# An attention and token/channel mixer kernel: the first batch written out by hand on three engines

## The chip, the cores and the metric

The kernel runs on one core of a Trainium2 chip. The metric is the device time of one execution in microseconds (us). Five engines take part: PE (matrix multiplications), DVE (VectorE), ACT (ScalarE), POOL (GpSimd) and SP, which here only issues DMA transfers. Each engine works through its own list of instructions in order and waits on semaphores for the others.

## The reference

Eight batches, 576 positions, 8 heads of 64. Attention runs inside chunks of 64 positions; its result x goes through a token mixer (along positions) and a channel mixer, each with a residual.

```python
# q, k, v: float32 (8, 8, 576, 64), in chunks of 64
scores = scale * np.matmul(q_c, k_c.transpose(0, 1, 2, 4, 3))
scores = scores - np.max(scores, axis=-1, keepdims=True)
attn = np.exp(scores)
attn = attn / (np.sum(attn, axis=-1, keepdims=True) + 1e-09)
out = np.matmul(attn, v_c)                    # -> x (8, 576, 512)
# w_tok1 (576, 256), w_tok2 (256, 576), w_ch1 (512, 1536), w_ch2 (1536, 512): float64
h = np.maximum(xt @ w_tok1, 0.0) @ w_tok2     # xt: x with positions last
u = x + h.transpose(0, 2, 1)
h2 = np.maximum(u @ w_ch1, 0.0) @ w_ch2
return u + h2
```

The four weight matrices arrive as float64 and are turned into float32 on the chip.

## The kernel before

**Tiles.** Two batches share nine attention tiles of 128 rows: batch 0 has five (the fifth is half its own, half batch 1's), batch 1 four, and so on in pairs. Per tile: scores (`attn_s`, L215, 32 small matmuls), on DVE a maximum (L223) and a subtraction (L225), on ACT the exponential (L229), a transposition of the probabilities `pr` to `pt`, the values with an added column of ones (`attn_v`, L276), and on DVE the division (`zi` L284 and L285, then `x` L287). The first batch transposes on PE (`near`, L254, copied by ACT at L267); later tiles go through a block transposition on DVE (L235), a DRAM buffer (`far`) and back (`pf`, `xt`).

**Mixers.** Of batch 0 the token mixer uses plain float32: `tok1_first` (L363) sums over the five tiles, a relu gives two halves of `r`, `tok2_first` adds the residual x to the same accumulator with identity matmuls (L378), multiplies `r` by the second weight (L385) and splits the result u into a rounded part `uh` (ACT, L389) and a remainder `ul` (DVE, L390). From there on, and in all later batches, a product of two float32 values is three matmuls of high and low parts (`THREE`). The channel mixer works on two halves of 288 positions in 12 steps: `ch1` (L432, 12 matmuls), the relu split into `gh` (ACT, L439) and `gl` (DVE, L440), and `ch2` (L459, 12 matmuls) into four accumulators, which step 11 adds to u (L466) and sends out. For batch 0, `ch1` of both halves runs in the first pass, with the second half's `gh` and `gl` kept; its `ch2` steps follow in a second pass. Batch 1 begins with `tok2` (L412).

**Weights.** A plan lists 31 pieces: three of the first token weight (t1), four of the second (t2), 24 of the channel weights (c1, c2 in turn, 512 columns each). A piece is fetched as pairs of 32-bit words (`fetch`, issued by SP), and converted by `convert_words`: two ACT passes (L138 the low words, L144 the magnitude of the high words), then on DVE a clamp (L145), a shift (L148), the sign (L152) and an addition (L156). `convert_split` rounds it to a high part on ACT (L170) and subtracts it on DVE (L171); the results are `kept_c` and `kept_t`. Batch 0's token mixer reads the float32 pieces (`tops`), the channel mixer and later batches read the split ones. The t pieces' splits are called in the second pass of batch 0.

**What sets the order.** SP's order is that of the program. For the first stage PE's order is too: the table `FIRST` says for each of seven steps how many weights to fetch, how many pieces to convert, and how many warming matmuls (L101, on zeros, results unused) to run ahead of the transposition and of `tok1_first`. DVE, ACT and POOL there, and every engine but SP afterwards, are ordered by a planner from its own estimates of durations. `qk` and `v` have three buffers each, so the load of the fourth tile waits for the first's to be free.

## Time and profile before

| what | value |
|---|---|
| median of three runs | 845.03 us (844.12 to 845.63) |
| the profiled execution | 846.61 us |
| its span in the trace | 844.8 us |
| mean granted clock of PE in it | 0.982 |
| PE busy | 824.5 us, 98% of the span |
| DVE busy | 358.1 us, 42% |
| ACT busy | 233.3 us, 28% |
| POOL busy | 116.4 us, 14% |
| first score matmul | 5.89 us |
| last x of batch 0 done | 49.34 us |
| first channel matmul | 63.95 us |
| last channel weight's remainder written | 113.40 us |
| first output addition of batch 0 | 135.84 us |
| first token-mixer matmul (L412) of batch 1 | 166.23 us |

A row of the profile names the line of the kernel (L276), the engine, the operation, what it writes and reads (out<-in) and how often it occurs; busy times are in us. Idle time of an engine is put down to what came last before it went on. Busy shares are averages over the whole span, so the stages are looked at one by one. The granted clock is 1.00 at full speed.

### The profile page before, as it was taken

How to read it: one execution, taken by the hardware profiler on the slowest of the kernel's cores; microseconds unless marked ns; L12 is line 12 of the kernel's file. 1: busy time of each engine (PE TensorE's matmuls, PEld its weight loads, DVE VectorE, ACT ScalarE, POOL GpSimd, SP SyncE). 2: the span in 40 equal slices, each digit the busy share in tenths (PEclk: the TensorE clock that was granted, in tenths of full speed). 3: DMA queues.
4: the chain of work that ended last, by engine and by line, in shares of the span. 5: the costliest groups of instructions: out<-in, count | busy, mean ns of one | idle time of the engine just before them, and what ended most of it. 6: DMA issues, size and time to landing. Idle time of an engine off the chain costs nothing.

```text
span 844.8 us, 18037 instructions
## 1 busy us (share of the span) xinstructions
PE 824.5 (98%) x7632; PEld 769.5 (91%) x7632; DVE 358.1 (42%) x762; ACT 233.3 (28%) x479; POOL 116.4 (14%) x133
## 2 busy tenths in 40 slices
PE   8689999999999999999999999999999999999997
PEld 5358999899998999999998999989999899999997
DVE  5989963253335334143433433243333434223121
ACT  4667731132223222132222322122222322212110
POOL 0000002220203002030201202030120302014000
PEclk8769999999999999999999999999999999999999
DMA  7891133323433233212433234202334223200000
GB/s 282 332 383 32 64 108 111 96 74 111 133 97 110 87 108 117 63 55 88 139 129 101 75 122 136 77 29 95 107 121 139 74 90 101 91 15 15 2 29 29
DMA packets 69985, 87.97 MB, mean 104 GB/s; under 512 B 8016, under 2 KB 48208, under 8 KB 69904
## 3 DMA queue, kind: packets, MB, share of 16 engines
q1 hardware_dynamic: 69904, 86.82, 31.2%
q8 instruction: 60, 0.98, 0.5%
q14 instruction: 21, 0.17, 0.1%
HBM read 59.92 MB, written 25.95 MB: 102 GB/s over the span
## 4 chain that ended last, share of the span: by engine, by line
PE 91%; DVE 4%; DMA 2%; ACT 2%; issue 0%; SPq 0%; DVEq 0%; ACTq 0%
PE acc L459 37%; PE ps_c L432 36%; PE ps_t L354 6%; PE ps_t L412 6%; PE ps_s L215 3%; PE ps_v L276 2%; DMA raw_t<-in_w 1%; DVE wtop L152 1%; PE ps_t L378 1%; DVE kept_c L171 1%; ACT low L138 1%; DVE wtop L145 1%; DVE wtop L156 0%; DMA raw_c<-in_wc 0%; DVE wtop L148 0%
## 5 line engine op out<-in xcount | busy, mean ns | idle before, releaser
L432 PE MATMUL ps_c<-uh,kept_c 128*128 128x288 f32 x1536 | 316.9, 296 | 0.0
L459 PE MATMUL acc<-gh,kept_c 128*128 128x288 f32 x1536 | 297.1, 297 | 1.4 <-ACT gh L439 1.3
L432 PEld LDWEIGHTS ps_c<-uh,kept_c 128*128 128x128 f32 x1536 | 247.0, 188 | 2.2
L459 PEld LDWEIGHTS acc<-gh,kept_c 128*128 128x128 f32 x1536 | 237.6, 188 | 5.8 <-ACT gh L439 2.9
L432 PE MATMUL ps_c<-ul,kept_c 128*128 128x288 f32 x768 | 226.4, 297 | 0.8 <-DVE ul L390 0.8
L440 DVE SCALAR_TENSOR_TENSOR gl<-ps_c,gh 128x288 fp32r<-128x288 f32 x192 | 86.9, 453 | 306.2 <-ACT gh L439 305.8
L459 PE MATMUL acc<-gl,kept_c 128*128 128x288 f32 x768 | 201.1, 296 | 0.0
L439 ACT ACTIVATE gh<-ps_c 128x288 fp32r<-128x288 f32 x192 | 78.8, 411 | 343.7 <-PE ps_c L432 332.4
L432 PEld LDWEIGHTS ps_c<-ul,kept_c 128*128 128x128 f32 x768 | 143.7, 188 | 1.4 <-DVE ul L390 1.0
L459 PEld LDWEIGHTS acc<-gl,kept_c 128*128 128x128 f32 x768 | 136.0, 189 | 0.8
L305 POOL TENSOR_TENSOR xl<-x,xh 128x512 fp32r<-128x512 f32 x28 | 36.8, 1313 | 401.4 <-ACT xh L304 387.1
L468 POOL TENSOR_TENSOR o<-o,ul 128x288 f32<-128x288 f32 x56 | 43.4, 803 | 234.0 <-DVE o L466 233.9
L412 PE MATMUL ps_t<-kept_t,rh 128*128 128x288 f32 x224 | 46.6, 302 | 0.0
L423 ACT CAST uh<-u 128x288 fp32r<-128x288 f32 x56 | 23.9, 432 | 47.8 <-DVE u L418 47.7
L354 PE MATMUL ps_t<-xh,kept_t 128*128 128x512 f32 x112 | 36.8, 405 | 0.0
L263 ACT COPY pt<-pf 128x512 f32<-128x512 f32 x31 | 19.2, 620 | 63.2 <-DMA pf<-far 63.2
L223 DVE TENSOR_REDUCE mx<-ps_s 128x8 f32<-128x512 f32 x36 | 24.8, 688 | 27.9 <-PE ps_s L215 27.8
L412 PEld LDWEIGHTS ps_t<-kept_t,rh 128*128 128x128 f32 x224 | 35.4, 188 | 1.0
L229 ACT ACTIVATE pr<-pr 128x512 f32<-128x512 f32 x36 | 22.7, 632 | 45.4 <-DVE pr L225 45.2
L215 PEld LDWEIGHTS ps_s<-qk 64*64 64x64 f32 x1152 | 24.1, 138 | 10.7 <-issue 8.4
L276 PE MATMUL ps_v<-v,pt 64*64 64x65 f32 x1152 | 26.9, 233 | 6.6 <-ACT pt L267 6.5
L412 PE MATMUL ps_t<-kept_t,rl 128*128 128x288 f32 x112 | 33.2, 301 | 0.0
(62 smaller groups left out, 631.2 us busy)
## 6 DMA issues: line engine op xcount, KB each, us to landing
qk<-in_qk SPq DMA_DIRECT2D x36, 512.0 KB, 3.9
far<-blocks SPq DMA_DIRECT2D x63, 256.0 KB, 2.1
raw_c<-in_wc SPq DMA_DIRECT2D x24, 512.0 KB, 9.5
v<-in_v SPq DMA_DIRECT2D x36, 260.0 KB, 4.2
out<-o SPq DMA_DIRECT2D x64, 144.0 KB, 1.9
pf<-far SPq DMA_DIRECT2D x124, 64.0 KB, 2.0
xt<-far SPq DMA_DIRECT2D x112, 64.0 KB, 2.0
raw_t<-in_w SPq DMA_DIRECT2D x4, 288.0 KB, 4.8
```

What stands on the lines that cost most here:

```text
L215: nc.tensor.matmul(ps[c * CH:(c + 1) * CH, a, hp * CH:(hp + 1) * CH], lhsT=qk[a * D:(a + 1) * D, 0, hp, c * CH:(c + 1) * CH], rhs=qk[a * D ...
L223: nc.vector.tensor_reduce(out=mx, in_=sv, axis=AX.X, op=ALU.max)
L276: nc.tensor.matmul(ps[c * CH:(c + 1) * CH, a, hp * DV:(hp + 1) * DV], lhsT=t["pt"][a * CH:(a + 1) * CH, hp, c * CH:(c + 1) * CH], rhs=t["v ...
L305: nc.gpsimd.tensor_tensor(out=xl, in0=t["x"], in1=xh.bitcast(F32), op=ALU.subtract)
L354: nc.tensor.matmul(ps, lhsT=lhsT, rhs=rhs, start=(n == 0 and q == 0), stop=(n == len(mt) - 1 and q == len(terms) - 1),)
L412: nc.tensor.matmul(ps[:, :HALF], lhsT=r[k][ri][:, m * P:(m + 1) * P], rhs=weights["t2", k, n][:, wi], start=(k == 0 and q == 0), stop=(k = ...
L423: nc.scalar.copy(out=uh[:, m], in_=u)
L432: nc.tensor.matmul(ps[:, :HALF], lhsT=weights["c1", f][:, wi, k * P:(k + 1) * P], rhs=u[ui][:, k], start=(k == 0 and q == 0), stop=(k == N ...
L439: nc.scalar.activation(out=gh, in_=ps[:, :HALF], func=AF.Relu)
L440: nc.vector.scalar_tensor_tensor(out=gl, in0=ps[:, :HALF], scalar=0.0, in1=gh.bitcast(F32), op0=ALU.max, op1=ALU.subtract)
L459: nc.tensor.matmul(accs[e], lhsT=weights["c2", f][:, wi, e * P:(e + 1) * P], rhs=g[gi], start=(f == 0 and q == 0), stop=(f == NFC - 1 and ...
L468: nc.gpsimd.tensor_tensor(out=o, in0=o, in1=u[1][:, e].bitcast(F32), op=ALU.add)
```

## The change

The first batch, up to the token mixer's first half, is written out in order for PE, ACT and DVE, not for PE alone. A generator, `conversion()`, yields one DVE step of the weight conversion at a time; the steps of two to three neighbouring pieces are interleaved (clamp of piece i, sign of piece i-1, shift of i, addition of i-1, remainder of i-2). `convert(n)` places the next n of them, and tables give the number at each place: `FIRST_FILL` per tile, `END_FILL` behind the last tile, `STEP_FILL` in the channel steps. `prepare` places the two ACT passes of a piece, and each such pass fetches the piece five further on (`AHEAD`). Warming matmuls go from 68 to 20.

Batch 0's x is transposed on PE into `xt` (copied by ACT), and batch 0 uses the general `tok2`, with DVE adding `xt` to the accumulator (`u`); the identity matmuls of `tok2_first` are gone. Tiles 0 to 4 get five buffers for `qk` and `v` of their own, later ones two. Steps that belonged to batch 1's attention are placed in the channel steps of batch 0 by a table of slots (`JOBS`, two slots per step in the first pass, one in the second). The seven splits of t pieces come at slots 25 to 31 and not ahead of the last instruction of the first pass on ACT and DVE. After the part written by hand the planner orders the three engines again, with nothing ahead of its end.

```diff
-FIRST = (
-    (2, 1, 0, 12),
-    (1, 1, 10, 2),
-    (2, 1, 8, 0),
-    (2, 1, 4, 0),
-    (2, 1, 4, 0),
-    (2, 1, 4, 4),
-    (1, 1, 0, 0),
-)
+AHEAD = 5
+WARM_T = (6, 2, 0, 0, 0)
+WARM_V = (0, 0, 0, 0, 0)
+FIRST_FILL = (3, 4, 5, 5, 6)
+PREPARE = (0, 2, 2, 2, 2)
+X_BEFORE = ((), (), (0,), (1,), (2,), (3, 4))
+END_FILL = (4, 3, 1)
+STEP_FILL = (5, 5)
+STARTS = ((10, 11, 13, 14), (15, 16, 18, 19), (20, 21, 24, 25), (25, 27, 30, 31))
+JOBS = [(9, "ready")]
+JOBS += [(s, "part", j, k) for j, ss in enumerate(STARTS) for k, s in enumerate(ss)]
+JOBS += [(25 + i, "split", i) for i in range(7)]
...
+    fetched = []
     def fetch(n):
-        for i in [j for _, j in zip(range(n), fetched)]:
+        for i in range(len(fetched), min(n, len(plan))):
+            fetched.append(i)
             key, src, lo, n = plan[i]
             nc.sync.dma_start(
                 out=raws[i][1].rearrange("p n w -> p (n w)"), in_=src[:, lo:lo + n].bitcast(I32)
             )
...
+    def words_scalar(i):
+        fetch(i + AHEAD)
+        n = plan[i][3]
+        st = raws[i][1]
+        tag, bufs = (f"wt{n}", token) if i < token else ("wt", 4)
+        tops[i] = pool.tile([P, n], F32, tag=tag, name="wtop", bufs=bufs)
+        lows[i] = pool.tile([P, DM], I32, tag="low", name="low", bufs=4)[:, :n]
+        nc.scalar.activation(out=tops[i], in_=st[:, :, 1].bitcast(F32), func=AF.Abs)
+        nc.scalar.activation(out=lows[i], in_=st[:, :, 0].bitcast(U32), func=AF.Copy, scale=2.0 ** -29)
...
+    prepared = []
+    def prepare(n=1):
+        for _ in range(n):
+            if len(prepared) < len(plan):
+                words_scalar(len(prepared))
+                prepared.append(len(prepared))
+    def conversion():
+        for i in range(len(plan) + 2):
+            if i < len(plan):
+                prepare(i + 1 - len(prepared))
+                words_clamp(i)
+                yield
+            if 0 < i <= len(plan):
+                words_sign(i - 1)
+                yield
+            if i < len(plan):
+                words_shift(i)
+                yield
+            if 0 < i <= len(plan):
+                words_add(i - 1)
+                if i - 1 >= token:
+                    split_high(i - 1)
+                yield
+            if token <= i - 2:
+                split_low(i - 2)
+                yield
...
-        qk = pool.tile([P, 2, NHP, P], F32, tag="qk", name="qk", bufs=3)
+        qk = pool.tile([P, 2, NHP, P], F32, tag="qk" if i > 4 else "qk0", name="qk", bufs=2 if i > 4 else 5)
...
+    def attn_p(i, fill=0):
+        t = tiles[i]
+        sv = t["s"]
         mx = pool.tile([P, 2, NHP, 1], F32, tag="mx", name="mx")
         nc.vector.tensor_reduce(out=mx, in_=sv, axis=AX.X, op=ALU.max)
-        pr = pool.tile([P, DM], F32, tag="pr", name="pr")
+        convert(fill)
...
+    def attn_o(i, fill=(0, 0)):
+        t = tiles[i]
+        pv = t["pv"]
         zi = pool.tile([P, 2, NHP, 1], F32, tag="zi", name="zi")
         nc.vector.tensor_scalar_add(out=zi, in0=pv[:, :, :, D:], scalar1=1e-9)
+        convert(fill[0])
         nc.vector.reciprocal(out=zi, in_=zi)
...
+            dst = xt[:, 4 * j:4 * j + (rows.stop - rows.start) // BK]
+            if ps is None:
+                far_in(tiles[t]["x"], dst, rows)
+            else:
+                nc.scalar.copy(
+                    out=dst.rearrange("p i n c -> p n i c"),
+                    in_=near(tiles[t]["x"], ps).rearrange("p (n q) -> p n q", n=NDT)[:, :, rows]
+                    .rearrange("p n (i c) -> p n i c", c=BK),
+                )
...
+            terms = [(r[k], tops["t2", k, n])] if b == 0 else [
+                (r[k][ri], weights["t2", k, n][:, wi]) for wi, ri in THREE
+            ]
...
+        while ("c1", f) not in weights:
+            convert(1)
...
+    by_hand = ExitStack()
+    by_hand.enter_context(tc.manual_schedule(engines=engines))
...
+    fetch(2)
     load_v(first[1])
-    with tc.manual_schedule(engines={nc.tensor.engine}):
-        warm(20)
-        sums = [ps_sum.tile([P, 512], F32, tag="sum", name="sum") for _ in range(NT1)]
-        for step, (weights_in, finish, warm_t, warm_x) in enumerate(FIRST):
-            i, j, k = step, step - 1, step - 2
-            fetch(weights_in)
-            if i + 2 < len(first):
-                attn_load(first[i + 2])
-            warm(warm_t)
-            if 0 <= j < len(first):
-                attn_t(first[j], ps_tr.tile([P, 512], F32, tag="t", name="ps_t"))
-            if i < len(first):
-                attn_s(first[i], ps_first, "first", far=False)
-            if 0 <= j < len(first):
-                attn_v(first[j], ps_first, "first", far=False)
-            warm(warm_x)
-            if 0 <= k < len(first):
-                tok1_first(k, sums)
-            convert(finish)
...
+    attn_load(first[2])
+    fetch(3)
+    attn_load(first[3])
+    fetch(5)
+    attn_load(first[4])
+    warm(12)
+    sums = [ps_sum.tile([P, 512], F32, tag="sum", name="sum") for _ in range(NT1)]
+    prepare()
+    attn_s(first[0], ps_first, "first")
+    last = len(first) - 1
+    for j in range(last + 1):
+        attn_p(first[j], 1)
+        if j:
+            attn_o(first[j - 1], (0, 1))
+        convert(FIRST_FILL[j])
+        for k in X_BEFORE[j]:
+            attn_x(0, first[k], transposed("x"))
+        warm(WARM_T[j])
+        attn_t(first[j], transposed("t"))
+        prepare(PREPARE[j])
+        if j < last:
+            attn_s(first[j + 1], ps_first, "first")
+        warm(WARM_V[j])
+        attn_v(first[j], ps_first, "first")
+        if j:
+            tok1_first(j - 1, sums)
+    convert(END_FILL[0])
+    attn_o(first[last], (1, 1))
+    convert(END_FILL[1])
+    tok1_first(last, sums)
+    r = [pool.tile([P, DM], F32, tag="gr", name="r", bufs=4) for _ in range(NT1)]
+    nc.scalar.activation(out=r[0], in_=sums[0], func=AF.Relu)
+    nc.vector.tensor_scalar_max(out=r[1], in0=sums[1], scalar1=0.0)
+    us = [
+        [pool.tile([P, NDT, HALF], F32R, tag=tag, name=tag) for tag in ("uh", "ul")] for _ in range(2)
+    ]
+    low = None
+    for m in range(NDT):
+        convert(END_FILL[2])
+        nxt = tok2(0, r, 0, m, us[0])
+        if low is not None:
+            low(nc.vector)
+        low = nxt
+    for k in X_BEFORE[last + 1]:
+        attn_x(0, first[k], transposed("x"))
+    convert(END_FILL[2])
+    low(nc.vector)
+    start_ps.close()
+    by_hand.close()
+    after = ExitStack()
+    for engine in engines:
+        ins = [i for i in nc.cur_bb.bb.instructions if i.engine == engine][-1]
+        after.enter_context(tc.issue_after(ins))
...
+    def part(j, k):
+        i = second[j]
+        if k == 0:
+            attn_s(i)
+            attn_p(i, 1)
+        elif k == 1:
+            attn_far(i)
+        elif k == 2:
+            attn_t(i)
+            attn_v(i)
+            attn_o(i)
+        else:
+            attn_end(i)
+            attn_x(1, i)
+            if j + 2 < len(second):
+                attn_load(second[j + 2])
+    def split(i):
+        with ExitStack() as late:
+            for engine in (nc.scalar.engine, nc.vector.engine):
+                late.enter_context(tc.issue_after(last_of[engine]))
+            split_high(i)
+            split_low(i)
...
+    kept, pend, accs = [], None, []
+    for f in range(NFC):
+        g = ch1(us[0], f)
+        convert(STEP_FILL[0])
+        extras(2 * f)
+        if f == 0:
+            for m in range(NDT):
+                tok2(0, r, 1, m, us[1])(nc.vector)
+        kept.append(ch1(us[1], f, kept=True))
+        convert(STEP_FILL[1])
+        extras(2 * f + 1)
+        if pend is not None:
+            ch2(*pend)
+        pend = (0, 0, us[0], f, g, accs)
+    ch2(*pend)
+    last_of.update({i.engine: i for i in nc.cur_bb.bb.instructions})
+    accs = []
+    for f in range(NFC):
+        if f >= NFC - 2:
+            r = (r if f == NFC - 1 else []) + [tok1(1, f - NFC + 2)]
+        ch2(0, 1, us[1], f, kept[f], accs)
+        extras(2 * NFC + f)
+    after.close()
+    attn_load(batch_tiles(2)[0])
+    attn_load(batch_tiles(2)[1])
...
```

DVE around the last two tiles of batch 0. First before, from the fifth tile's maximum (`mx`) on; `wtop` is a piece under conversion, `raw_` a fetched one.

```order
L223 TENSOR_REDUCE mx<-ps_s 128x8
L156 ISA wtop<-wtop,low 128x1024 x2
L145 TENSOR_SCALAR wtop<-wtop 128x512
L284 TENSOR_SCALAR zi<-ps_v 128x8
L152 SCALAR_TENSOR_TENSOR wtop<-raw_c_2_164,wtop 128x512
L225 TENSOR_TENSOR pr<-ps_s,mx 128x2x4x64
L171 TENSOR_TENSOR kept_c_1_763<-wtop,kept_c_1_763 128x512
L148 TENSOR_SCALAR wtop<-wtop 128x512
```

And of the changed kernel, the fifth tile's maximum, with the fourth tile's `zi` and x behind it:

```order
L274 TENSOR_REDUCE mx<-ps_s 128x8
L158 TENSOR_SCALAR wtop<-wtop 128x288
L277 TENSOR_TENSOR pr<-ps_s,mx 128x2x4x64
L345 TENSOR_SCALAR zi<-ps_v 128x8
L347 RECIPROCAL zi<-zi 128x8
L173 ISA wtop<-wtop,low 128x576
L352 TENSOR_TENSOR x<-ps_v,zi 128x512
```

Between the maximum and the subtraction one conversion step is left, and no remainder of a channel piece has been computed by then; this maximum is row 43 of DVE's order, where it was row 67.

ACT around the third tile's copy of the transposed probabilities, before (`raw_t`, `raw_c` are fetched pieces, `low` and `wtop` what the two passes write):

```order
L138 ACTIVATE low<-raw_t_1_1_180 128x288
L144 ACTIVATE wtop<-raw_t_1_1_180 128x288
L138 ACTIVATE low<-raw_c_0_176 128x512
L144 ACTIVATE wtop<-raw_c_0_176 128x512
L267 COPY pt<-ps_t 128x512
L170 CAST kept_t_1_1_2117<-wtop 128x288
```

And now:

```order
L281 ACTIVATE pr<-pr 128x512
L399 COPY xt<-ps_x 128x4x4x32
L318 COPY pt<-ps_t 128x512
L148 ACTIVATE wtop<-raw_t_0_1_184 128x288
L149 ACTIVATE low<-raw_t_0_1_184 128x288
```

The copy of the third tile comes right behind its exponential and one copy of x, ahead of the passes over pieces 5, 6 and 7.

DVE in the token mixer's first half, which the program now sets step by step (`r` is the relu of the second half, `u` the sum, `ul` its remainder):

```order
L584 TENSOR_SCALAR r<-sum 128x512
L158 TENSOR_SCALAR wtop<-wtop 128x512
L471 TENSOR_TENSOR u<-ps_t_674,xt 128x288
L173 ISA wtop<-wtop,low 128x1024
L471 TENSOR_TENSOR u<-ps_t_686,xt 128x288
L477 TENSOR_TENSOR ul<-u,uh 128x288
L223 TENSOR_TENSOR kept_c_1_655<-wtop,kept_c_1_655 128x512
```

Each u stands behind one conversion step, and each ul behind the next u.

More of the change, by code (lines that the diff above doesn't have):

```diff
@@ L178, in convert_split, with convert @@
             weights[key] = parts
[L180 to L182 removed]
+    vector_ops = conversion()
+    def convert(n):
         for _ in range(n):
[L184 to L189 removed]
+            next(vector_ops, None)
     tiles = {}
@@ L366, in tok1_first @@
             )
-    def tok2_first(n, dst, r):
-        uh, ul = dst
-        lo, hi = n * HALF, (n + 1) * HALF
-        accs = [ps_acc.tile([P, 512], F32, tag="acc", name="ps_t2")[:, :HALF] for _ in range(NDT)]
-        for m, ps in enumerate(accs):
-            begun = False
-            for t, rows, j in mix_tiles(0):
-                a, z = max(lo, j * P), min(hi, j * P + rows.stop)
-                if a < z:
-                    nc.tensor.matmul(
-                        ps[:, a - lo:z - lo], lhsT=tiles[t]["x"][:, m * P:(m + 1) * P],
-                        rhs=ident[:, a - j * P:z - j * P], start=not begun, stop=False,
-                    )
-                    begun = True
-        for m, ps in enumerate(accs):
-            for k in range(NT1):
-                nc.tensor.matmul(
-                    ps, lhsT=r[k][:, m * P:(m + 1) * P], rhs=tops["t2", k, n],
-                    start=False, stop=(k == NT1 - 1),
-                )
-            nc.scalar.copy(out=uh[:, m], in_=ps)
-            nc.vector.tensor_tensor(out=ul[:, m], in0=ps, in1=uh[:, m].bitcast(F32), op=ALU.subtract)
     def tok1_end(ps):
@@ L445, in ch2 @@
     def ch2(b, n, u, f, g, accs):
+        while ("c2", f) not in weights:
+            convert(1)
         if f == 0:
@@ new lines, in split, with extras @@
+    def split(i):
[4 more added lines that the diff above has]
+            split_low(i)
+    last_of = {}
+    extra = {}
+    for slot, job, *of in JOBS:
+        extra.setdefault(slot, []).append((job, of))
+    def extras(slot):
+        for job, of in extra.get(slot, ()):
+            {"ready": ready, "part": part, "split": split}[job](*of)
```

171 lines of the change are left out of this document (68 added, 103 removed).

## The prediction

> **What bounds the kernel now.** I read the stages first (busy time of each engine in seven stretches of the profiled execution), then the waits, then the timelines around the longest waits, then the shapes and spacings of VectorE's work. The columns of the first view are the stretch, its length, and for each engine busy time and instructions; then the granted clock, the DMA share and GB/s.
>
> ```profile
> core 0: us, PE busy (x) PEld busy (x) DVE busy (x) ACT busy (x) POOL busy (x), PEclk, DMA share, GB/s
> 0.00:5.89 5.89, 4.82 (x20) 2.85 (x20) 0.18 (x1) 1.44 (x2) 0.70 (x6) 1.00 0.72 226
> 5.89:49.34 43.45, 30.64 (x405) 19.11 (x404) 37.82 (x92) 27.27 (x53) 0.00 (x0) 0.76 0.89 335
> 49.34:63.95 14.61, 14.55 (x76) 10.28 (x76) 11.29 (x24) 8.57 (x16) 0.00 (x0) 0.65 0.92 357
> 63.95:80.89 16.94, 14.85 (x99) 13.31 (x98) 16.94 (x38) 12.23 (x26) 0.00 (x0) 1.00 0.13 39
> 80.89:135.84 54.95, 54.95 (x531) 52.36 (x530) 41.04 (x86) 27.10 (x54) 4.56 (x3) 1.00 0.23 73
> 135.84:166.23 30.39, 30.39 (x265) 27.13 (x263) 8.04 (x17) 3.08 (x6) 5.23 (x7) 1.00 0.37 116
> 166.23:844.80 678.57, 674.27 (x6248) 644.49 (x6244) 242.83 (x510) 153.64 (x326) 105.88 (x118) 1.00 0.27 86
> ```
>
> The cuts are: the first score matmul (5.89), the end of the last x of batch 0 (49.34), the first channel matmul L432 (63.95), PE gapless from 80.89, the first output addition L466 of batch 0's first half (135.84), the first token-mixer matmul L412 of batch 1 (166.23). From 166.23 PE idles 4.3 us in 678.6, and the matmuls of batches 1 to 7 are untouched by the change, so anything it gives or takes is decided before 166.23. There the first stretch is the odd one: PE 30.64 of 43.45 us and the clock 0.76, while VectorE works 37.82. VectorE's conversion goes on past the last x, to the last subtraction L171 of a channel weight at 113.40:
>
> ```profile
> 49.34:113.40 64.06, 61.91 (x483) 54.20 (x484) 60.55 (x128) 41.84 (x81) 1.98 (x1) 0.92 0.34 121
> ```
>
> VectorE idles 5.6 us in the first stretch and 3.5 in the second. The waits up to 114 us (VectorE) and 166 us (PE), columns: total, times, longest:
>
> ```profile
> DVE wtop L145 <- ACT wtop L144: 10.3, 5, 6.0
> DVE ul L390 <- ACT uh L389: 3.3, 1, 3.3
> PE ps_v L276 <- ACT pt L267: 6.5, 3, 4.4
> PE ps_t L254 <- ACT pr L229: 4.6, 3, 2.4
> ```
>
> The 4.4 us is readable in the timelines (start, duration, operation; in brackets the idle time before):
>
> ```profile
> 25.63 0.45 ACT L144 ACTIVATE wtop<-raw_t 128x288 f32<-128x288 f32 x1
> 28.37 0.66 ACT L138 ACTIVATE low<-raw_c 128x512 int32<-128x512 uint32 x1 [2.29 <-DMA raw_c<-in_wc]
> 29.48 0.58 ACT L267 COPY pt<-ps_t 128x512 f32<-128x512 f32 x1
> 24.44 0.66 PE L254 MATMUL ps_t<-ident,pr 128*128 128x128 f32 x4 [2.35 <-ACT pr L229]
> 30.11 0.70 PE L276 MATMUL ps_v<-v,pt 64*64 64x65 f32 x14 [4.38 <-ACT pt L267]
> ```
>
> PE's transposes ended at 25.1, but ScalarE sat on a weight that had not landed, and the copy of the transposed tile stood behind it. So the stage is bound by in-order queues: attention steps of one tile stand behind conversion steps that are not urgent. At the last x VectorE had done far more conversion than token mixing needs.
>
> **The change, term by term.** VectorE's spacings come from starts in its timeline, where neighbours do not depend on each other:
>
> ```profile
> 47.47 0.68 DVE L171 TENSOR_TENSOR kept_c<-wtop,kept_c 128x512 fp32r<-128x512 f32 x1
> 48.07 0.68 DVE L152 SCALAR_TENSOR_TENSOR wtop<-raw_c,wtop 128x512 int32<-128x512 int32 x1
> 48.67 0.67 DVE L287 TENSOR_TENSOR x<-ps_v,zi 128x512 f32<-128x512 f32 x1
> 49.27 0.41 DVE L148 TENSOR_SCALAR wtop<-wtop 128x512 int32<-128x512 int32 x1
> 49.61 0.68 DVE L152 SCALAR_TENSOR_TENSOR wtop<-raw_c,wtop 128x512 int32<-128x512 int32 x1
> 65.54 0.45 DVE L390 TENSOR_TENSOR ul<-ps_t,uh 128x288 fp32r<-128x288 f32 x1
> 65.91 0.68 DVE L156 CUSTOM_DVE_ANT_0 wtop<-wtop,low 128x1024 uint16<-128x1024 uint16 x1
> 66.51 0.42 DVE L145 TENSOR_SCALAR wtop<-wtop 128x512 f32<-128x512 f32 x1
> 51.14 0.70 DVE L235 STREAM_TRANSPOSE blocks<-x 128x512 f32<-128x512 f32 x1
> 51.77 0.64 DVE L152 SCALAR_TENSOR_TENSOR wtop<-raw_c,wtop 128x512 int32<-128x512 int32 x1
> ```
>
> A full two-operand step of 512 columns advances VectorE 0.60 us (47.47 to 48.07; L156 65.91 to 66.51 too), a clamp or shift 0.34 (49.27 to 49.61), a step of 288 columns 0.37 (65.54 to 65.91), a stream transpose 0.63. A conversion piece with its subtraction is 4 rows + 1 = 0.34+0.34+0.60+0.60+0.60 = 2.48 us.
>
> The Trainium skill, page "VectorE: DVE Perf Modes", section "The DRAIN you can't avoid", says that a next step starts only when the pipe of the last is empty; its note on unheld neighbours allows an earlier start. The trace sides with the latter (0.68 long, 0.60 apart). By the strict rule each of the rows counted next would be some 0.08 longer, 169 of them 13 us, and the forecast would move to about 844.
>
> *Ahead of the last x* the changed order has 63 rows on VectorE (38 of conversion, 25 of attention) where 92 stood. By the spacings (each 256- or 288-column step in proportion) they sum to 24.0 us; the same sum for the 92 rows gives 37.2 against 37.82 measured, so I scale to 24.4. The first score matmul can start once 12 instead of 20 warming matmuls have run: 8 x 0.24 (4.82/20) earlier, 3.97 us; I take 4.5 for the landing of qk, bounds 3.97 and 5.89. The first reduction follows 0.75 later, 5.25. With no idle VectorE would end the last x at 29.7. It idled 5.6 us in this stretch before; I take 4.9, because the first weight lands no sooner while the stall behind ScalarE goes: **last x at 34.5 instead of 49.34.** PE would allow this: per tile the x transposes (0.66, as L254), transposes 0.66, scores 0.69, values 0.70 and the token matmuls 1.98 make 4.7 us at full clock, five of them 23.5. At half clock the rows below are 1.6 times as long (values 1.08 against 0.70, tokens 3.11 against 1.98), a tile 7.5, and the first two, without token matmuls, about 4.7; with the 8 us of VectorE rows behind the last tile's subtraction and 1.5 for its scores and reduction, 4.5 + 9.4 + 15 + 9.5 puts the last x near 39. Lower bound 29.7, upper bound 39.
>
> ```profile
> 36.79 0.52 PE L215 MATMUL ps_s<-qk 64*64 64x64 f32 x23
> 38.04 1.98 PE L363 MATMUL sum<-x,wtop 128*128 128x512 f32 x4
> 43.16 1.08 PE L276 MATMUL ps_v<-v,pt 64*64 64x65 f32 x32 [0.67 <-ACT pt L267]
> 49.40 3.11 PE L363 MATMUL sum<-x,wtop 64*128 64x512 f32 x4 [1.62 <-DVE x L287]
> 52.44 5.33 PE L378 MATMUL ps_t<-ident,x 128*128 128x128 f32 x24
> ```
>
> *From the last x to the last channel-weight subtraction* VectorE now has 169 rows where 128 stood: 86 of conversion (22+22 at 0.60, 42 at 0.34: 40.5 us), 24 subtractions (14.4), 23 gl at 0.37 (8.5), 8 new u additions and 8 ul (5.9), six stream transposes (3.8), the attention steps of three tiles, r and the stack (6.4): 79.5, scaled 80.0, against 60.55. This is the debt of the first stage, paid later. The seven kept_t subtractions (3.3 us) leave this chain for the second half, where VectorE works 8.04 of 30.39 us; so they and the seven casts cost nothing, and 3.3 us if they came back.
>
> To the 80.0 comes idle time. Before, it was 3.5 in this stretch. Now the token-mixer rows are written out in VectorE's order (u waits for PE, then ul for ScalarE, with one conversion step between): PE's last four token matmuls (3.11 at half clock, 1.98 full), relu (0.7) and the first L466 pair stand between, filled by about four conversion rows. I take 2 us at full clock, 7 at half, and 0 to 4 for waits on gh in the channel steps; together 5.0. **Last subtraction at 34.5 + 80.0 + 5.0 = 119.5**, before 113.40. So conversion ends later, and this is the point on which the change turns: PE no longer arrives last.
>
> PE's own line: last x 34.5, then 7.5 for token matmuls, relu and half the token mixer (the 24 identity matmuls L378, 5.33 us at half clock for the first half, are gone), then what stood between 63.95 and 135.84, 14.85 + 54.95 = 69.8 busy with the other half's identity matmuls in it, at most 69.8: 111.8. That is ahead of VectorE's 119.5, so VectorE sets the end, and PE idles some 8 us in the channel steps. After the last subtraction come twelve matmuls (1.6 us) and the addition: **first output addition at 121.5**, before 135.84: 14.3 us earlier. Before, 22.4 us lay between these two points, all PE work (113.40 to 135.84); this slack is what the change spends.
>
> From there 30.39 us to batch 1 as before: PE was gapless there, and its matmuls are the same. Batch 1's attention parts move by slot numbers; they need VectorE and the far round trip inside the first half, counted above.
>
> Fetches: 24 channel pieces of 512 KB; a piece takes 1.28 us at 410 GB/s and VectorE needs one every 80.0/24 = 3.3 us. So pacing costs nothing; without this cover (a fetch issued only as its predecessor's predecessor is consumed) a piece would cost its 9.5 us landing once.
>
> ```profile
> raw_c<-in_wc SPq DMA_DIRECT2D x24, 512.0 KB, 9.5
> 37.00:43.00 6.00, 4.07 (x67) 2.22 (x56) 6.00 (x14) 4.93 (x9) 0.00 (x0) 1.00 1.03 411
> 50.00:61.00 11.00, 11.00 (x56) 7.89 (x55) 7.89 (x15) 5.06 (x10) 0.00 (x0) 0.53 1.03 409
> ```
>
> SP issues the tiles' loads ahead of channel weights, and five buffers take away its wait on a free one; behind its waits on consumed pieces stand only later pieces and batch 1's loads.
>
> **Sum.** The profiled execution took 846.61 us (span 844.80, 1.8 around it), 1.6 above the median of the runs, 845.03. 846.6 - 14.3 = 832.3 for a profiled execution, 830.7 by the median. I say 831.
>
> The last quoted row is the clock's: at 50 to 61 us PE was busy without a gap and still at 0.53. The Trainium skill, "TensorE: Matmul & The Clock Gate", Part 1, gives about 3.4 us of sustained work until full speed. Here some 10 us passed. By that page of the Trainium skill the idle time taken as 5.0 would be nearer 2, giving 828; by the row nearer 9, giving 835.
>
> **Rivals.** *(a) VectorE hardly idles.* The stall behind ScalarE was the largest single one (4.4 us) and hand order removes it; last x at 33.7, 1 us of idle: last subtraction 114.7, output addition 116.5, 19 us won, **825** (with 29.7 as the last x, 821). Against it: the first conversion step cannot start before the first weight has landed.
>
> *(b) The clock stays half.* Fewer warming matmuls (20 instead of 68) and gaps per tile; in this stage the mean was 0.76 with them. Last x at 39, 10 us of idle: last subtraction 129, addition 131, 5 us won, **840**. Against it: VectorE, not PE, limits a tile, and the added x transposes fill gaps.
>
> *(c) Slower: channel steps go in lockstep.* VectorE's 23 gl rows stand at fixed places between conversion rows; each waits for twelve matmuls (1.6) and ScalarE's gh (0.41, mean 411 ns). If PE in turn waits for that step's weight, each costs up to 2 us. It decides from 0.85 us each: 23 x 0.85 = 19.5, when the last subtraction passes 134 and the addition 135.84. At 1.0 each: 34.5 + 80 + 2 + 23 = 139.5, addition 141.5, **850.7**. For it: VectorE is the late engine now. Against: in the order some 30 rows separate a weight's subtraction from the first gl that needs it early on, 7 at the end, and PE is the faster one.
>
> ```profile
> L439 ACT ACTIVATE gh<-ps_c 128x288 fp32r<-128x288 f32 x192 | 78.8, 411 | 343.7 <-PE ps_c L432 332.4
> ```
>
> *(d) The change only moves the stall:* the last x comes at about 45 since weights or qk land as before, and the later 80 us eat the rest: 45 + 80 + 7 = 132, addition 134, **844 to 845**.
>
> **Numbers.** Forecast 0.50 (827 to 837), (a) 0.22 (821 to 827), (b) 0.16 (837 to 843), (c) 0.07, (d) 0.05. About 0.2% (1.7 us) can be told from no change. Faster: 0.50+0.22+0.16 = 0.88; same 0.05; slower 0.07. Range 822 to 841: the forecast, most of (a) and about half of (b); it takes in the bounds of the last x with the idle time taken.
>
> **What would show it.** Last x near 34 and 63 rows ahead of it; last subtraction near 119 with VectorE busy above 90% from the last x on; PE idle in the channel steps of the first half with waits on kept_c; first output addition 2 us behind the last subtraction; 30 us from there to batch 1; 678 us after that. Wrong: PE gapless in the channel steps (then PE still bounds), VectorE idle over 15 us after the last x (lockstep), or a difference arising after batch 1's start.

## The result

The changed kernel takes 830.14 us (median, 828.99 to 831.20) against 845.33 us (844.12 to 845.72) of the kernel before in the same comparison: a ratio of 0.9822 with a 95% interval of 0.9803 to 0.9842, so 1.8% faster. A second comparison gave 830.08 us and 0.983 (0.9813 to 0.9847). The forecast was 831 us. The profiled execution took 831.20 us, with a span of 829.4; it is the slowest of the four. A second profile of the same kernel (831.26 us) has the last x 0.4 us later, the last channel remainder 1.5 earlier and the first output addition within 0.1, so differences of that size between two profiles mean little. One execution further down, the profiled one of the run that fetches all weights at once, took 1957 us where its three others took 833, and is not counted.

The busy times of the changed kernel, cut at the same events as before (first score matmul, end of the last x of batch 0, first channel matmul, first output addition, first token-mixer matmul of batch 1):

```profile
core 0: us, PE busy (x) PEld busy (x) DVE busy (x) ACT busy (x) POOL busy (x), PEclk, DMA share, GB/s
0.00:4.49 4.49, 3.06 (x12) 1.64 (x12) 0.18 (x1) 1.28 (x1) 0.70 (x6) 1.00 0.53 197
4.49:33.75 29.26, 22.94 (x376) 14.99 (x376) 24.42 (x64) 19.02 (x37) 0.00 (x0) 0.83 1.03 399
33.75:44.27 10.52, 8.58 (x29) 5.31 (x29) 7.57 (x17) 4.63 (x11) 0.00 (x0) 0.84 1.03 409
44.27:120.72 76.45, 71.14 (x604) 66.19 (x605) 73.85 (x154) 50.96 (x101) 3.25 (x2) 0.96 0.33 109
120.72:150.84 30.12, 29.67 (x274) 26.59 (x272) 13.53 (x27) 5.02 (x11) 8.78 (x9) 1.00 0.24 75
150.84:829.40 678.56, 674.87 (x6264) 645.12 (x6264) 245.15 (x510) 154.00 (x327) 105.57 (x117) 1.00 0.28 89
```

The whole gain lies ahead of the last x. It ended at 49.34 us and now ends at 33.75, 15.6 earlier. From there to the first output addition it is 87.0 us (86.5 before), from that to batch 1 30.1 (30.4 before), and the rest takes 678.56 (678.57). The 15.6 us are VectorE's 13.4 us less work in that stretch (24.42 for 37.82), a start 1.4 earlier, and 0.8 less idle time (4.8 for 5.6).

That the third part is as long as before hides an exchange. VectorE is now busy 81.4 of the 87.0 us (7.57 + 73.85); up to its last channel remainder it works 81.1 of 86.0 us, where it was 60.55 of 64.06. Before, 22.4 us of PE work lay between that remainder and the addition, now one microsecond. It is not the last remainder that PE waits for, though. VectorE finishes the remainder of the last c1 piece at 114.91 (first row); PE has waited 1.4 us for it, and from there on runs without a gap to the addition, 5.8 us later. The last remainder, of c2, ends at 119.71, just as PE gets to the matmuls of that piece (last of PE's rows). VectorE's timeline (start, duration, in brackets the idle time before), then PE's:

```profile
114.23 0.68 DVE L223 TENSOR_TENSOR kept_c<-wtop,kept_c 128x512 fp32r<-128x512 f32 x1
118.20 0.44 DVE L495 SCALAR_TENSOR_TENSOR gl<-ps_c,gh 128x288 fp32r<-128x288 f32 x1
119.02 0.69 DVE L223 TENSOR_TENSOR kept_c<-wtop,kept_c 128x512 fp32r<-128x512 f32 x1 [0.38 <-ACT kept_c L217]
119.63 0.45 DVE L495 SCALAR_TENSOR_TENSOR gl<-ps_c,gh 128x288 fp32r<-128x288 f32 x1
120.72 1.55 DVE L523 TENSOR_TENSOR o<-acc,uh 128x288 f32<-128x288 f32 x4 [0.64 <-PE acc L516]
```

```profile
114.97 0.40 PE L487 MATMUL ps_c<-uh,kept_c 128*128 128x288 f32 x1 [1.40 <-DVE kept_c L223]
119.72 0.83 PE L516 MATMUL acc<-gh,kept_c 128*128 128x288 f32 x5
```

PE's waits up to batch 1 (total, times, longest) show the same: the single wait of 4.4 us behind ScalarE's copy is gone, waits are at most 2.2 us, and waits for channel weights (`kept_c`) have come in.

```profile
PE ps_v L333 <- ACT pt L314: 2.9, 2, 2.1
PE ps_t L305 <- ACT pr L281: 2.7, 2, 2.2
PE ps_c L487 <- ACT xt L399: 1.9, 1, 1.9
PE ps_v L333 <- ACT pt L318: 1.6, 2, 0.8
PE ps_c L487 <- DVE kept_c L223: 1.4, 1, 1.4
PE acc L516 <- ACT kept_c L217: 0.9, 1, 0.9
```

### The profile page after: what moved, and what is told of

The parts are those of the page before. It is cut to its first block, busy times and chain, and to the rows that moved or that the text cites. A ratio compares the mean times of both kernels' runs of the same rounds, so it can differ in the third digit from the quotient of the medians.

```text
span 829.4 us, 17900 instructions
## 1 busy us (share of the span) xinstructions
PE 810.3 (98%) x7556; PEld 759.8 (92%) x7556; DVE 364.7 (44%) x770; ACT 234.9 (28%) x484; POOL 118.3 (14%) x133
## 4 chain that ended last, share of the span: by engine, by line
PE 88%; DVE 8%; DMA 1%; issue 1%; ACT 1%; SPq 0%; DVEq 0%; ACTq 0%
PE acc L516 36%; PE ps_c L487 34%; PE ps_t L466 6%; PE ps_t L428 6%; PE ps_s L262 3%; PE ps_v L333 2%; DVE wtop L165 1%; DVE wtop L173 1%; DVE kept_c L223 1%; DMA raw_t<-in_w 1%; DVE wtop L152 1%; DVE gl L495 1%; PE sum L437 1%; DVE wtop L158 1%; DVE mx L274 0%
## 5 line engine op out<-in xcount | busy, mean ns | idle before, releaser
L516 PE MATMUL acc<-gl,kept_c 128*128 128x288 f32 x768 | 204.1, 297 | 0.0
L476 ACT CAST uh<-u 128x288 fp32r<-128x288 f32 x64 | 26.7, 432 | 46.2 <-DVE u L471 46.1
L471 DVE TENSOR_TENSOR u<-ps_t,xt 128x288 f32<-128x288 f32 x64 | 28.0, 451 | 17.1 <-PE ps_t L466 16.0
L477 POOL TENSOR_TENSOR ul<-u,uh 128x288 fp32r<-128x288 f32 x35 | 29.6, 855 | 20.5 <-ACT uh L476 20.1
```

Source lines behind the costliest of these rows:

```text
L471: nc.vector.tensor_tensor(out=u.rearrange("p (i c) -> p i c", c=BK), in0=ps[:, :HALF].rearrange("p (i c) -> p i c", c=BK), in1=xt[:, n * H ...
L476: nc.scalar.copy(out=uh[:, m], in_=u)
L477: return lambda engine: engine.tensor_tensor(out=ul[:, m], in0=u, in1=uh[:, m].bitcast(F32), op=ALU.subtract)
L516: nc.tensor.matmul(accs[e], lhsT=weights["c2", f][:, wi, e * P:(e + 1) * P], rhs=g[gi], start=(f == 0 and q == 0), stop=(f == NFC - 1 and ...
```

## The experiments

The theory: from the last x on two lines run, VectorE's conversion and PE's matmuls, and the later one sets the first output addition; after the change that is VectorE's. All runs change the changed kernel. The table gives each run's median time, the end of the last x, the end of the last channel subtraction, the first output addition, and the time from the last x to that addition, all but the median from the profiled execution. Behind the change the addition follows the last subtraction by 0.8 to 14.6 us: the last subtraction does not by itself say which line ended last, PE's waits do.

| run | us | last x | last subtraction | addition | x to addition |
|---|---|---|---|---|---|
| before | 845.33 | 49.34 | 113.40 | 135.84 | 86.5 |
| changed | 830.14 | 33.75 | 119.71 | 120.72 | 87.0 |
| changed again | 830.08 | 34.17 | 118.21 | 120.76 | 86.6 |
| clamp twice | 841.30 | 34.05 | 125.61 | 129.50 | 95.5 |
| clamp left out | 828.49 | 33.60 | 106.12 | 115.53 | 81.9 |
| more matmuls | 833.62 | 33.95 | 118.82 | 120.31 | 86.4 |
| 27 steps back | 845.38 | 51.92 | 118.64 | 133.27 | 81.4 |
| piece by piece | 834.34 | 36.16 | 118.85 | 122.97 | 86.8 |
| kept_t early | 834.94 | 36.35 | 121.21 | 124.43 | 88.1 |
| all at once | 833.37 | | | | |
| POOL subtracts | 833.75 | 34.49 | 121.57 | 122.38 | 87.9 |
| identity matmuls | 832.01 | 34.26 | 119.71 | 120.79 | 86.5 |
| more warming | 831.08 | 33.58 | 119.23 | 120.25 | 86.7 |
| identity, placed early | 828.82 | 33.76 | 115.29 | 116.89 | 83.1 |

**VectorE's work doubled at one step, and taken away.**

```diff
     def words_clamp(i):
-        nc.vector.tensor_scalar(
-            out=tops[i], in0=tops[i], scalar1=LEAST, scalar2=MOST, op0=ALU.max, op1=ALU.min
-        )
+        for _ in range(2 if i >= 10 else 1):
+            nc.vector.tensor_scalar(
+                out=tops[i], in0=tops[i], scalar1=LEAST, scalar2=MOST, op0=ALU.max, op1=ALU.min
+            )
```

> The clamp of pieces 10 to 30 is issued twice (the second changes nothing): 21 more VectorE steps behind the last x of batch 0, 21 x 0.34 = 7.1 us, up to 9 with the second waiting for the first. Theory (VectorE's conversion sets the first output addition): that addition moves from 120.7 by 6 to 9 us to 127 to 130, and the time from 830.1 to 836 to 839. Rival (PE still sets it, VectorE follows): VectorE has some 5 us of idle time in that stretch, so the time stays within 830 to 833.

```diff
     def words_clamp(i):
+        if i >= 10:
+            return
         nc.vector.tensor_scalar(
```

> The clamp of pieces 10 to 30 is left out (very small and very large weights would be converted wrongly): 21 VectorE steps fewer, 7.1 us. Theory: the first output addition comes earlier until PE is in the way; PE idles 5.3 us between the first channel matmul (44.3) and that addition, so 4 to 6 us are won: 824 to 826. Rival (PE sets it): 829 to 831, nothing won.

Twice: 841.30 us, ratio to the kernel before 0.9955 (0.994 to 0.9969); the addition 8.8 us later for 7.1 us of work, as expected, but the median 11.2 longer, above the 836 to 839 expected; 1.9 us of that lie behind batch 1's start. Left out: 828.49 us, 0.9803 (0.978 to 0.9826); the addition 5.2 us earlier, as expected, the profiled execution, its fastest, 4.1 shorter (827.07), but the median only 1.7, short of the 824 to 826 expected. Both move the addition as VectorE's line says, and the second shows where PE's line begins: the last subtraction came 13.6 us earlier, but the addition stopped 81.9 us behind the last x, with PE at full clock and 69.0 of 71.8 us busy (first row; the second is the doubled clamp).

```profile
43.72:115.53 71.81, 69.02 (x607) 64.35 (x608) 66.73 (x134) 50.98 (x102) 2.65 (x2) 1.00 0.36 115
45.09:129.50 84.41, 74.71 (x621) 68.26 (x622) 79.64 (x174) 51.85 (x102) 5.03 (x2) 0.94 0.30 98
```

With the doubled clamp VectorE's last subtraction came only 5.9 us later. PE waited seven times, 8.2 us in all, for channel weights; the last of these waits ended at 115.52, and PE then ran without a gap up to the addition, 6.0 us of it at half clock (PE's waits from 33 to 130 us: total, times, longest):

```profile
PE acc L517 <- ACT kept_c L218: 2.8, 2, 1.5
PE ps_c L488 <- ACT kept_c L218: 2.6, 2, 1.8
PE ps_c L488 <- DVE kept_c L224: 1.6, 2, 0.8
PE acc L517 <- DVE kept_c L224: 1.2, 1, 1.2
```

**PE's work raised.**

```diff
+                for _ in range(dose[0] if k == 0 and q == 0 else 0):
+                    nc.tensor.matmul(
+                        ps[:, :HALF], lhsT=weights["c1", f][:, wi, :P], rhs=u[ui][:, k],
+                        start=True, stop=True,
+                    )
```

(`dose[0]` is 2 in the first pass of batch 0 and 0 elsewhere.)

> Two more matmuls of 288 columns ahead of each of the 24 channel groups ch1 of batch 0 (their result is overwritten by the group's own first matmul): 48 x 0.134 = 6.4 us of PE work. Theory (VectorE sets it): they fall into PE's 5.3 us of idle time; the first output addition moves by 0 to 3 us, 830 to 833. Rival (PE sets it): all 6.4 are paid, 836 to 837.

The addition came at 120.31, 0.4 us earlier than in the changed kernel: the 6.4 us vanished in PE's idle time, as the theory says. That time is used up by them: between first channel matmul and addition PE idled 0.9 us (5.3 in the changed kernel), and from 71.76 on not at all. The time is nevertheless 833.62 us, 3.5 above the changed kernel, just outside the theory's range and well short of the rival's. In the profiled executions 1.8 us separate the two, the slowest of four for the changed kernel and the fastest of four here; 1.6 of them lie between the addition and batch 1 (31.76 us for 30.12), where the planner put the steps in another order.

**The deferred steps put back ahead of the last x.**

```diff
-END_FILL = (4, 3, 1)
+END_FILL = (31, 3, 1)
```

> 27 conversion steps go back ahead of the last x of batch 0 (END_FILL 31 instead of 4), so that 90 VectorE rows stand there as in the kernel before (92); all else as changed. They take 27 x 0.48 = 13 us: last x at about 47 instead of 33.8. Theory: the last subtraction stays near 120, PE's line becomes the later one: 47 + 10.5 for the token mixer + 66 to 71 of PE work = 123 to 128 for the first output addition, 833 to 838. Rival (the deferral is worth nothing, the gain is the order's and the freed waits'): 829 to 831. Rival (the last x alone sets the time): 13 us lost, 842 to 844.

845.38 us, ratio 1.0004 (0.999 to 1.0017): the gain is gone, more than the theory's 833 to 838 and than the second rival's 842 to 844. The last x came at 51.92, not 47: of the 18.2 us that it moved, 13.9 are VectorE's work and 4.0 idle time, so the steps put back in this place cost more than their work. Without these 4.0 us the time would be near 841 (an estimate, 845.4 less 4.0). In a row, the five steps of a piece took 3.3 to 3.6 us, 0.7 to 1.0 of it waiting for ScalarE's pass over the piece; in VectorE's timeline from one clamp to the next:

```profile
44.07 0.43 DVE L152 TENSOR_SCALAR wtop<-wtop 128x512 f32<-128x512 f32 x1 [0.70 <-ACT wtop L148]
...
47.63 0.43 DVE L152 TENSOR_SCALAR wtop<-wtop 128x512 f32<-128x512 f32 x1 [0.99 <-ACT wtop L148]
```

And the stages of this run (last x to first channel matmul, then to the addition):

```profile
51.92:63.79 11.87, 11.01 (x29) 6.45 (x29) 7.55 (x17) 4.53 (x10) 0.00 (x0) 0.65 0.22 74
63.79:133.27 69.48, 67.14 (x603) 63.21 (x604) 60.44 (x127) 41.42 (x84) 2.81 (x2) 1.00 0.21 68
```

The last subtraction came at 118.64, 14.6 us ahead of the addition, so PE's line ended last: 51.92 + 11.87 + 69.48. Together with the run without clamps PE's line measures 81.4 to 81.9 us from the last x; VectorE's, in the changed kernel, 87.0. With the last x at 33.75 PE could have added at 115.4, about 5 us earlier than it did.

**The steps of one piece behind one another; the token splits early.**

```diff
                 words_clamp(i)
                 yield
-            if 0 < i <= len(plan):
-                words_sign(i - 1)
-                yield
-            if i < len(plan):
                 words_shift(i)
                 yield
...
+                words_sign(i)
                 yield
...
+                words_add(i)
```

> The conversion generator gives clamp, shift, sign and addition of one piece one behind the other (only the remainder still lags by one piece); counts per place and all else as changed. In the kernel before, a dependent step started 0.34 to 0.49 us behind its predecessor where independent ones of the same width took 0.23 to 0.37: 0.11 more, three times per piece. Theory: 10 pieces (3 us) ahead of the last x, partly inside waits, 21 (7 us) behind; last x 34 to 37, last subtraction 126 to 130, time 837 to 841. Rival (the pipe empties between any two steps, so order inside the stream is free): 829 to 832.

```diff
-                if i - 1 >= token:
-                    split_high(i - 1)
+                split_high(i - 1)
...
-JOBS += [(25 + i, "split", i) for i in range(7)]
```

> The seven splits of token pieces go back into the conversion stream (ScalarE's cast and VectorE's subtraction right behind the addition), out of the second pass; the number of stream steps at each place stays. 3.3 us of VectorE work return to the chain up to the last channel subtraction. Theory (VectorE sets the first output addition, and more than its own time is paid, as with the doubled clamp: 8.8 for 7.1): addition 3 to 5 us later, 833 to 835. Rival (hidden in VectorE's idle time or behind PE): 829 to 831.

Piece by piece: 834.34 us, 0.987 (0.9854 to 0.9885), 4.2 above the changed kernel. Ahead of the last x the theory held: dependent steps start only when the one before has ended (0.84 us from start to start in the next two rows, where 0.60 is usual), and the last x came 2.4 us later.

```profile
7.82 0.69 DVE L165 SCALAR_TENSOR_TENSOR wtop<-raw_t,wtop 128x512 int32<-128x512 int32 x1
8.66 0.69 DVE L173 CUSTOM_DVE_ANT_0 wtop<-wtop,low 128x1024 uint16<-128x1024 uint16 x1
```

Behind it neither held: the last subtraction came at 118.85, 82.7 us behind the last x (86.0 in the changed kernel). There the planner is free to set other rows between, and the trace shows that it does: ahead of the last x 17 conversion steps start only behind the end of the step before, behind it 3, and none in the changed kernel. The addition followed the last x by 86.8 us even so (87.0), with PE idle for 7.6 us of it behind the first channel matmul. Token splits early: 834.94 us, 0.9876 (0.9857 to 0.9895), inside the theory's range, but by another way. The addition moved by 3.7 us, 2.6 of them ahead of the last x; the addition followed 88.1 us behind that. Ahead of the last x VectorE works as long as in the changed kernel (24.5 us) but idles 2.3 us more: ScalarE's casts of token pieces stand ahead of its copies of the transposed probabilities, PE waits 4.5 us for these copies (1.6 in the changed kernel), and VectorE 7.4 us for scores (5.3).

**All weights fetched at once; POOL subtracts.**

```diff
-AHEAD = 5
+AHEAD = 31
```

> All 24 channel pieces are fetched right behind the tiles' loads (AHEAD 31), ahead of batch 1's loads, not five pieces ahead of use. Theory: a piece takes 1.28 us to fetch and 3.3 to convert, so nothing changes: 829 to 832. Rival (pacing keeps the queue free for what is urgent): batch 1's loads and the stack land up to 20 us later and hold up its scores, which are placed in the channel steps: 834 or more.

```diff
-        nc.vector.tensor_tensor(
+        (nc.gpsimd if i >= 12 and i % 3 == 0 else nc.vector).tensor_tensor(
             out=parts[:, 1], in0=tops[i], in1=parts[:, 0].bitcast(F32), op=ALU.subtract
```

> Seven of the 24 channel remainders (pieces 12, 15, ... 30) are subtracted by POOL, idle in this stretch, not by VectorE: 4.2 us less on VectorE, 1.3 us instead of 0.68 for each of the seven. Theory: first output addition 2 to 4 us earlier (leaving out 7.1 us of clamps gave 5), 826 to 828. Rival (each weight comes 0.7 us later and PE waits for it, or the two engines slow each other): 830 to 833.

All at once: 833.37 us, 0.9857 (0.9838 to 0.9875), between the two expectations. Where the 3 us lie stays open. In the trace of its profiled execution, where a piece landed every 1.28 us as in the changed kernel, SP issued batch 1's first loads behind all 24 pieces and they landed from 52.7 us on, for 33.5 in the changed kernel, as the rival expected; whether that is the reason was not tested. POOL: 833.75 us, 0.9865 (0.985 to 0.9881), the rival's case. VectorE was relieved of seven steps and worked no less: 75.11 us between first channel matmul and addition, for 73.85. POOL's timeline, then VectorE's, at two of the seven:

```profile
68.09 1.79 POOL L223 TENSOR_TENSOR kept_c<-wtop,kept_c 128x512 fp32r<-128x512 f32 x1 [9.54 <-ACT kept_c L217]
78.95 1.30 POOL L223 TENSOR_TENSOR kept_c<-wtop,kept_c 128x512 fp32r<-128x512 f32 x1 [9.07 <-ACT kept_c L217]
```

```profile
68.65 1.52 DVE L158 TENSOR_SCALAR wtop<-wtop 128x512 int32<-128x512 int32 x1
79.12 1.67 DVE L165 SCALAR_TENSOR_TENSOR wtop<-raw_c,wtop 128x512 int32<-128x512 int32 x1
```

A shift of 0.41 us took 1.52 and a sign step of 0.68 took 1.67: each ended 0.3 to 0.5 us behind POOL's step. The last channel remainder, one of the seven, ended at 121.57. The Trainium skill, "SBUF — State Buffer", section "Who interferes with whom", says that VectorE and GpSimd share a pair of ports that one instruction holds to its end while the other blocks; this trace agrees, with 0.6 to 1.1 us lost at each of six POOL steps, 5.1 us in all; at the seventh VectorE had no such step.

**The control.** The unaltered changed kernel beside the next two.

> The changed kernel itself, unaltered, beside the two below: if the steps of 3 to 5 us that several small edits cost are theirs, it takes 829 to 831.5 again; if they are the chip's or the day's, 833 or more.

It took 830.08 us, so the 3 to 5 us are the edits'.

**The residual by identity matmuls, and more warming.**

```diff
+        if b == 0:
+            nc.scalar.copy(out=uh[:, m], in_=ps[:, :HALF])
+            return lambda engine: engine.tensor_tensor(
+                out=ul[:, m], in0=ps[:, :HALF], in1=uh[:, m].bitcast(F32), op=ALU.subtract
+            )
...
-X_BEFORE = ((), (), (0,), (1,), (2,), (3, 4))
+X_BEFORE = ((), (), (), (), (), ())
```

(with the 12 identity matmuls of a half ahead of its products, as in `tok2_first` before)

> Batch 0's token mixer adds the residual again by identity matmuls into the accumulator, as in the kernel before, in the new hand order: no x transposes on PE, no copies into xt on ScalarE, and none of the eight u additions on VectorE (8 x 0.37 = 3.0 us); PE gets the 24 identity rows back. Theory (VectorE sets the first output addition, PE has some 7 us to spare): first channel matmul 1 to 2 us earlier (no wait for xt, 1.9 us), first output addition 2 to 4 us earlier, 826 to 828. Rival (PE's added rows or the other order of the channel steps cost as much): 830 to 834.

```diff
-WARM_T = (6, 2, 0, 0, 0)
+WARM_T = (16, 7, 3, 0, 0)
```

> 18 more warming matmuls in the first three tiles (16, 7, 3 instead of 6, 2, 0), put into PE's idle time of 2.2, 0.5 and 0.8 us there, where the clock was at half from 8 to 19 us. Theory (VectorE and the landing of weights limit a tile, not PE's clock): last x within 1 us of 33.8, 829 to 832. Rival (the half clock holds the tiles up): PE's work from 8 to 19 us, 8.9 us, shrinks to about 5, the last x comes 2 to 3 us earlier and so does everything behind it, 827 to 828.

Identity: 832.01 us, 0.9855 (0.9831 to 0.9879), the rival's range; the addition did not move (120.79). The identity rows stood behind the last token matmuls and PE, at half clock, took 4.5 us for the first half's; VectorE, rid of the u additions, waited as long for the first ul (PE's row, then VectorE's):

```profile
36.22 4.49 PE L463 MATMUL ps_t<-ident,x 128*128 128x128 f32 x24
```

```profile
42.23 0.46 DVE L485 TENSOR_TENSOR ul<-ps_t,uh 128x288 fp32r<-128x288 f32 x1 [4.28 <-ACT uh L484]
```

Warming: 831.08 us, 0.9838 (0.9817 to 0.9859). The clock was full from 10.3 us to the last x, where the changed kernel had half from 8.0 to 18.2, and the last x came 0.2 to 0.6 us earlier. That half clock had cost next to nothing. (The first row's 1.00 holds from 10.3 us only, where this trace's records of the clock begin; ahead of that the first scores took 1.13 us and a warming matmul 0.25, for 0.70 and 0.15 in the changed kernel, so PE was at half speed.)

```profile
4.70:33.58 28.88, 24.27 (x394) 15.92 (x394) 24.47 (x64) 18.98 (x37) 0.00 (x0) 1.00 1.03 399
```

In its PE timeline the first scores, the 16 warming matmuls and the second scores, at 0.70 us (1.13 in the changed kernel):

```profile
4.70 1.13 PE L262 MATMUL ps_s<-qk 64*64 64x64 f32 x32 [0.57 <-DMA qk<-in_qk]
5.76 4.02 PE L108 MATMUL ps_w<-warm_in 128*128 128x288 bf16 x16
10.48 0.70 PE L262 MATMUL ps_s<-qk 64*64 64x64 f32 x32
```

**Both lines shortened.** The same run with the identity matmuls moved into PE's wait for the last x, and seven conversion steps in VectorE's wait.

```diff
+    begun = [tok2_begin(0, m) for m in range(NDT)]
     convert(END_FILL[0])
     attn_o(first[last], (1, 1))
...
-        convert(END_FILL[2])
+        convert(END_FILL[2] if m else 7)
```

> The run with the identity matmuls, with two places changed. The 12 identity rows of the first half stand ahead of the last token matmuls, in PE's wait for the last x (2.3 us there), not behind them, where they took 4.5 us at half clock and VectorE waited 4.3 us for the first ul; and seven conversion steps, not one, stand ahead of that first ul. The x transposes, the xt copies and the eight u additions are gone as before. Theory (two lines from the last x, the later one ends: VectorE's rows plus its idle time, 86.9 us in the changed kernel, and PE's token mixer plus 69.5 to 71.8): last x 34, VectorE's rows 80.0 - 3.0 = 77 and 2 us of idle time, so a last subtraction at 113; first channel matmul at 41 to 43, PE's line at 112 to 114; first output addition 113 to 116 and the time 823 to 826. Rival (each edit of the order costs 3 to 5 us in the channel steps whatever it saves): 830 or more.

The mechanism held, the size was less: first channel matmul at 41.95 (44.27), last subtraction at 115.29, addition at 116.89, 3.8 us earlier than in the changed kernel. VectorE idled 4.1 us up to its last subtraction, where 2 were expected. PE's last wait of more than 0.1 us ended at 97.84, so PE's line came last. PE had no wait for the last x any more, kept its full clock, and took 2.76 us for the identity rows and 1.98 for the last token matmuls:

```profile
31.39 2.76 PE L463 MATMUL ps_t<-ident,x 128*128 128x128 f32 x24
34.08 1.98 PE L437 MATMUL sum<-x,wtop 64*128 64x512 f32 x4
```

The time is 828.82 us, 0.9806 (0.9787 to 0.9824), the lowest of the kernels that compute everything; against the changed kernel's 830.1 that is 1.3 us, with intervals that overlap. That is within neither expectation: short of the theory's 823 to 826, below the rival's 830. The profiled executions differ by more, 3.3 us (827.94 and 831.20 or 831.26), but the former is the fastest of its five and the latter are each the slowest of four, so the medians are the fairer comparison.

## Why the prediction was right

The numbers of its chain, forecast and measured: last x 34.5 and 33.75; VectorE's rows from there to its last subtraction 80.0 and 81.1; its idle time there 5.0 and 4.9; last subtraction 119.5 and 119.7; first output addition 121.5 and 120.7; to batch 1 30.4 and 30.1; after that 678.6 both. The small misses cancel: the last x 0.75 early, VectorE's work 1.1 long.

- **Ahead of the last x**: 24.4 us of VectorE's work and 4.9 idle were forecast, 24.42 and 4.84 measured. That the reason is the deferred steps, and not the freed waits, two things show: 13.4 of the 15.6 us are VectorE's work, and with 27 steps put back no gain is left. That run takes away somewhat more than the deferral, 4.0 us of idle time that its own order makes. The stall behind ScalarE's copy is gone, but VectorE's idle time in the stretch differs by no more than 0.8 us. The five buffers of `qk` and `v` were not tested by themselves.
- **The last step was right in part by luck.** The prediction lets PE wait for the last subtraction and then do twelve matmuls, 2 us up to the addition; 1.0 was measured. But PE waits for the remainder of the last c1 piece, 5.8 us ahead of the addition, and the last remainder is there when PE gets to it. In the second profile of the changed kernel it came at 118.21, 2.5 us ahead of an addition at the same place.
- **VectorE sets the end**: shown by more and less VectorE work, and by PE work that costs nothing up to the addition. "PE idles some 8 us in the channel steps" was too much: 5.3 us idle, and a clock of 0.96 that used up part of the rest. PE's own line, worked out as at most 77.3 us behind the last x, measures 81.4 to 81.9; the token-mixer term (7.5 for 10.1 to 11.9) was mis-sized most. PE's slack is thus 5 us and not 9.7. Less VectorE work than that would be paid back only in part, as the run without clamps shows.
- **The token splits cost nothing in the second pass**: VectorE works 13.53 of 30.12 us there. The price given for undoing it, 3.3 us, was too low (4.9), and 2.6 us of it are paid through a later last x, which the prediction did not see.
- **Pacing costs nothing**: agrees with the trace (no channel weight is late); that fetching all at once costs 3 us was not foreseen and is not explained.
- **Rivals.** (a) needed VectorE to idle 1 us between the last x and its last subtraction; it idled 4.9. (b) half clock throughout: the clock was half from 8.0 to 18.2 us, and the run with more warming shows that this cost at most 0.6 us. The Trainium skill's 3.4 us of sustained work ("TensorE: Matmul & The Clock Gate", Part 1): in the run with more warming PE worked without a gap from 4.70 and the clock was full 5.6 us later, which the page allows, as its window does not start with the work; the kernel before, with more than 10 us of work at half clock, does not agree, and the measured time stands. The idle time came out between the two sums. (c) lockstep: VectorE waited once for a gh and twice for a cast, 1.4 us in all. With its work raised by 7.1 us the addition moved by 8.8, with PE's waits and its half clock near the end, so the coupling is there, but small at the changed kernel's own load. (d) the last x at 45 did not come; by its own sum (addition at 134) this rival gives 843.2, not 844 to 845, and (a) gives 825.7, not 825.
- **The strict pipe rule** of the Trainium skill ("VectorE: DVE Perf Modes", "The DRAIN you can't avoid") would have put the time near 844. VectorE's independent steps kept starting 0.60 apart, and the run with dependent neighbours shows what the rule describes: 0.84.
- **What stays open.** Two small edits (more matmuls, POOL's subtractions) cost 3.5 and 3.6 us in the median though the first output addition moved by -0.4 and 1.7. In the profiled executions 1.6 and 1.0 us more lie between that addition and batch 1, and 0.6 and 0.5 behind batch 1's start, where neither edit adds or takes an instruction; why was not tested.

## What to carry to other kernels

When two engines both start from one event, here the last x, ask for each how long its line is from there. Work that one engine defers past the event brings the event and the other engine's line forward, and is free until the first engine's own line is the longer one. Here that point is passed: VectorE's line is some 5 us longer than PE's, of 87, so deferring more would gain nothing; less work on VectorE gains up to these 5 us, and more than that needs both lines shortened. And a count from an order written out by hand, times spacings measured in the trace, plus the idle time that a like stretch had, gave the length of a stage of 30 and of 87 us to 1 us, the second with some luck at its end.

## What the runs showed of the hardware that was not expected

- A POOL subtraction of 1.3 us stretched the VectorE step beside it by 0.6 to 1.1 us (shift 0.41 to 1.52, sign step 0.68 to 1.67), so that work moved from VectorE to POOL did not relieve it.
- A full clock in the tile stage from 10.3 us on did not shorten it by more than 0.6 us. A PE wait of 2.3 us ahead of the last token matmuls was followed by a half clock: the identity rows took 4.49 us there and 2.76 where no wait stood ahead. The length of a wait alone does not decide it: behind the same wait of 1.40 us for the last c1 remainder the mean clock up to the addition was 1.00 in one profile of the changed kernel and 0.77 in the other.
- A VectorE step that reads the result of the one just ahead of it started 0.84 us behind it, one that does not 0.60; order alone was worth 1.9 us of VectorE's busy time ahead of the last x (26.29 for 24.42).
